# Third attention batch's loads moved to GpSimd's queue, behind the first expert's second weight matrix, with the front's order drawn up anew

## The chip, the core and the metric

The kernel runs on one core of one Trainium2 chip. The metric is the device time of one execution in microseconds (us). A core has five engines that run their own instruction lists side by side: TensorE (PE, matrix multiply), VectorE (DVE), ScalarE (ACT), GpSimd (POOL) and SyncE (SP, here only a queue that issues transfers). Transfers are issued either from SP or from GpSimd and are carried out by 16 DMA engines that all queues share.

## The reference, cut to what matters

Linear attention (8 batches, 8 heads, 576 positions, head width 64) makes the tokens, and a mixture of 8 experts works on them. The gate weights are normalised by eight Sinkhorn rounds over all 4608 tokens, so they are known only when the last batch is through attention.

```python
phi = lambda x: np.where(x > 0, x, np.exp(x) - 1.0) + 1.0
q_p, k_p = phi(q), phi(k)
kv  = einsum('bhsd,bhse->bhde', k_p, v);  z = sum(k_p, axis=2)
x   = einsum('bhsd,bhde->bhse', q_p, kv) / (einsum('bhsd,bhd->bhs', q_p, z) + 1e-6)
# x is laid out as N = 4608 tokens of D = 512
P = exp(x @ w_gate - max);  8 times: P /= row sums;  P /= column sums;  P *= N / E
for e in range(8):                       # F = 1024
    out += P[:, e:e+1] * (maximum(x @ w1[e], 0) @ w2[e])
```

## The kernel before

The kernel has a front and a long main part. The front (about the first 200 us) runs the attention of the 8 batches, two half batches `n = 2b + g` for each batch, and fills TensorE's gaps with expert 0, group by group of 512 tokens (`hq` is the first layer, `ye` the second). The main part runs experts 1 to 7 with a seven-product block scheme.

Nothing is ordered by hand. The program is a list of tasks; a small planner inside the kernel (`_Plan`) gives each engine a fixed order when the kernel is built. It uses written-in durations (here 6.0 for a whole weight matrix) and a table of priorities, `ranks`, which may also pin a copy to ACT or DVE. What the chip then executes is a fixed list for each engine.

The loads. A weight matrix is float32 in memory and is cast to float16 by the transfer; only GpSimd issues it:

```python
def load_w(ten, nm, pl, ap, cut, e, prio, parts=1, after=0.0, deps=()):
    ...
    for i in range(parts):
        def fn(_, i=i):
            ...                                     # part i of the matrix
            nc.gpsimd.dma_start(out=dst, in_=AP(tensor=ten.tensor, offset=off, ap=a))
        ti = add(("pool", 1.0), fn, use=[g], prio=prio, deps=[tal])
        ts_.append(add(("dma", 6.0 / parts), lambda _: None, deps=[ti], use=[g], prio=prio, lat=2.6))
        w_last[0] = ti
```

The inputs of a half batch (`k`, `q`, `v`, 576 KB each; two buffers for each of the three):

```python
for nm, ten in (("k", k), ("q", q), ("v", v)):
    def fn(_, gr=gr, nm=nm, ten=ten):
        gr["tile"] = fp.tile([P, 2, NJ, D], FP32, tag=nm + "in", name=nm + "in", bufs=2)
        (nc.gpsimd if n in (2, 3) else nc.sync).dma_start(...)
    ti = fadd(("pool", 1.0) if n in (2, 3) else ("sp", 0.45), fn, acq=[gr], prio=pr,
              deps=[w_last[0] if n in (2, 3, 4) else None, in_prev[0]])
...
att(0, 0); att(0, 1)
w_t = {0: load_w1(0, prio=-290.0, parts=2, deps=[gates[0]])}
for b in range(1, B):
    att(b, 0); att(b, 1)
    if b == 1:
        w_t[0] += load_w2(0, prio=-96.5, parts=2, deps=[in_prev[0]])
    if b % 2 == 1:
        logits(b // 2)
add(("pool", 0.8), f_wg, prio=-90.0, deps=[w_last[0]])     # w_gate, 8 KB
```

One half batch then runs: `ek`, `eq` (exponentials, ACT), `tk`, `tq` (DVE), `vv` (a cast, ACT or DVE), and on TensorE `kv_ps`, `qt_ps` (transposes of q), `den_ps`, `num_ps`, `xt_ps` (transposes of the result into `xT`), with DVE or ACT copies between them (`kvz`, `qpT`, `rden`, `xn`, `xT`). The small matrix products use one pair of PSUM buffers in turn (`att`).

The second layer of expert 0 needs one half of w2 for the first four of its eight products, the other for the last four:

```python
for half in range(2):
    for f in range(4 * half, 4 * half + 4):
        nc.tensor.matmul(gy[tt]["tile"], lhsT=gh["tile"][:, f, ds(P * tt, P)], rhs=gw2["tile"][:, f, :], ...)
    ty[tt] = add(("pe", 0.87), f_y, deps=[tw2[half], ty[tt]] + ..., ...)
```

In the built program GpSimd issues the half with rows `f` 4 to 7 first and the half with rows 0 to 3 second, before and after the change alike; TensorE wants rows 0 to 3 first.

At the start, 47 products on a tile of zeros (`yw <- warm`) keep TensorE occupied while there is no other work.

Of the kernel before, what the change touches and what calls it, by code (L numbers as in the profile page):

```python
# [122 lines left out]
def kernel(  # L123
# [10 lines left out]
    nc = tc.nc  # L134
# [17 lines left out]
    add = S_.add  # L152
# [41 lines left out]
    def load_w(ten, nm, pl, ap, cut, e, prio, parts=1, after=0.0, deps=()):  # L194
        g = S_.grp(pl)
        ts_ = []
# [4 lines left out]
        for i in range(parts):  # L201
            def fn(_, i=i):
                dst, a, off = g["tile"], [list(x) for x in ap], e * DM * F
                if parts > 1:
                    n = a[cut][1] // parts
                    off += i * n * a[cut][0]
                    a[cut][1] = n
                    dst = dst[:, i * n:(i + 1) * n, :] if cut == 1 else dst[:, :, i * n:(i + 1) * n]
                nc.gpsimd.dma_start(out=dst, in_=AP(tensor=ten.tensor, offset=off, ap=a))
            ti = add(("pool", 1.0), fn, use=[g], prio=prio, deps=[tal])  # L210
            ts_.append(add(("dma", 6.0 / parts), lambda _: None, deps=[ti], use=[g], prio=prio, lat=2.6))
            w_last[0] = ti
# [21 lines left out]
    def fadd(*a, **kw):  # L234
        t = add(*a, **kw)
        front_ids.append(t)
        return t

    def att(b, g):
        n = 2 * b + g  # L240
# [9 lines left out]
        for nm, ten in (("k", k), ("q", q), ("v", v)):  # L250
            gr = gin[nm] = S_.grp(p_in[nm])

            def fn(_, gr=gr, nm=nm, ten=ten):
                gr["tile"] = fp.tile([P, 2, NJ, D], FP32, tag=nm + "in", name=nm + "in", bufs=2)
                (nc.gpsimd if n in (2, 3) else nc.sync).dma_start(
                    out=gr["tile"].rearrange("p r j d -> p r (j d)"),
                    in_=AP(tensor=ten.tensor, offset=(b * H + 4 * g) * S * D, ap=src))
            ti = fadd(("pool", 1.0) if n in (2, 3) else ("sp", 0.45), fn, acq=[gr], prio=pr,
# [666 lines left out]
    for tt in (3, 2, 1, 0):  # L925
# [5 lines left out]
        0:8.9853 36:-98.0084 38:-98.0036 40:-98.021 42:-85.0117 43:-85.0126 44:-98.0219 45:-85.0096  # L931
        46:-98.0036 47:-98.0147 49:-85.0105:act 50:9.0018 51:-98.0201 52:-98.0087 54:-85.0123 55:9.0204:dve
        56:-85.0102 57:8.9967:dve 58:8.9967 59:-98.0183 61:-85.0111 62:8.9928 63:-98.0015 64:8.9928
        65:-98.0039 66:-85.0066 67:-85.0105 68:-85.0126:act 69:-85.0096 70:-98.0054:dve 71:-85.0081
        73:8.9976 75:-98.0006 77:-98.0015 78:-98.0204 79:-85.009 80:8.9946 81:-85.0117 82:-98
        84:-85.0111:dve 85:-98.0165 86:8.9991 88:9.0003 89:-85.0006 90:-85.0084 91:-85.0087:act 92:-98.0105
        93:8.9916 95:8.9934 96:8.9979 97:-98.0081 98:-85.0087 99:-98.018 100:-85.0105 101:-85.009
        102:-98.0054 103:-85.0072 104:-98.0195 106:-97.9991 108:8.9934 110:-98.0042 112:-98.0165 114:8.994
        116:-98.0081 117:-98.0366 118:-98.009 119:-85.0108 120:-98.0216 121:-85.009 123:-85.0108
        124:-98.0084 125:-85.0126 127:-98.0042 128:-98.0036:act 129:8.9928 130:-98.018:dve 131:-85.0117  # L940
        132:-98.003 134:-98.0072 135:-85.0099 136:-98.0153 137:9.0153 138:-85.0099 139:-98.0051 140:-98.0315
        141:-98.0021:dve 142:-98.0081 143:-98.0024 144:-98.0183 146:-85.0132 148:8.9991 150:-98.0072
        151:8.9952 152:9.0189 153:-85.0099 154:-85.0075 155:-98.0105 157:8.9925:act 158:-98.0336
        159:-85.0132 161:-98.0093 162:-85.0084 163:-98.0321 164:-98.0093 165:8.9889 166:-98.0081
        168:-85.0138 169:-98.0153 170:-98.0078 171:-98.0156 172:-98.0081 173:-98.0084 174:-98.0168
        175:-98.0327:act 176:-98.0123 177:-85.0105:act 179:-85.0102 181:-98.0045 183:8.9943 184:-98.0054
        185:-85.0141 187:-98.0096 189:8.9913 191:-98.0153 192:-98.0039 193:-85.0096 194:-98.0069 195:9.0174
        196:9.0192 198:8.9937 199:-98.0033 200:-85.0078 202:-85.0117 203:-98.0075:act 204:-98.0012
        205:-98.0222 206:-85.0147 207:-98.0111 209:-98.0243 210:-85.0132 211:7.6305 212:-85.0084 213:9.0072
        214:-98.0066 215:-98.015 216:-85.0084 217:-97.9949 218:-85.0078 219:-85.009 221:-85.0075  # L950
        223:-85.0081 225:-98.0177 226:8.9943 227:-98.0342 228:-85.0105 229:9.0192 230:-98.0081
        232:8.9934:act 233:-98.0102 234:-98.0069 236:-85.0132 237:-98.0339:dve 238:-85.0063 239:-98.0078:act
        240:-98.0063 241:8.9928 243:-85.0093 244:8.9907 245:8.9853 246:-98.0075 247:-98.015 248:-98.0357
        249:-98.0156 250:-85.0138 251:-98.0159 252:-85.0117 253:-98.009 255:-85.0111 257:-98.0099
        259:-98.0054 260:-98.0123 261:8.9916 262:-85.0135 263:-98.0054 264:8.9994 266:-98.009:dve 267:8.9931
        268:-98.0123 270:-85.0216 271:-98.0345:act 272:-85.0141 273:-85.009:act 274:-85.0078 275:-85.0129
        277:-98.015 278:-98.0108 279:8.9928 280:-98.0135 281:-98.0186 282:8.9904 283:8.9931 284:-85.0126:act
        285:-98.012 286:-85.0072:act 287:-98.0084 289:8.9952 291:-85.0066 293:-85.0099 294:-97.9958
        295:-85.0126 296:8.9892 297:-85.0072 298:-98.0051 300:8.9943:dve 301:-98.0138 302:8.9862
        304:-98.0156 305:-98.018 306:-85.0219 307:-98.012:act 308:-85.0099 309:8.9916 311:8.9859  # L960
        312:-98.0192 313:-98.0111 314:-85.0108 315:8.9913 316:8.9904 317:8.9952 318:-85.003:dve 319:-85.0099
        320:8.994:dve 321:-85.012 322:-85.0021 323:9.0195 325:-98.0327 327:-98.0249 329:-98.03 330:-85.0075
        331:9.0198 332:-98.0054 333:-85.0069 334:-98.0201 336:-98.0177:act 337:8.9874 338:-98.0108
        340:-85.0204 341:-85.0099 342:8.9925 343:8.9895 344:-85.0069 345:9.0078 347:-98.0222 348:-85.0126
        349:-85.0144 350:-85.0081 351:-98.0249 352:-85.0159 353:-98.0021 354:-98.0141:act 355:8.9874
        356:-98.015:act 357:9.0057 359:-85.0132 361:-85.0078 363:-85.0054 364:8.9889 365:-98.0114
        366:-85.006 367:-85.0156 368:-85.0093 370:8.9904:dve 371:9.0153 372:-85.0126 374:-85.0042 375:8.994
        376:8.9913 377:8.997:act 378:7.6314 379:-85.0114 381:8.9931 382:-85.0096 383:-98.0174 384:-85.012
        385:-98.0147 386:-85.0081 387:-98.0237 388:-85.0114:act 389:-98.0015 390:-98.0141:act 391:-98.0315
        393:-98.0222 395:8.9904 397:-98.0045 398:8.9985 399:-85.0135 400:-98.0168 401:8.9874 402:-85.0111  # L970
        404:-98.0138:act 405:8.9895 406:-97.9976 408:-85.0027 409:-85.0087:dve 410:-98.0024 411:-85.0087
        412:-85.0126 413:-98.0165 415:-98.0021 416:-85.012 417:-98.006 418:-98.0132 419:-85.0204 420:8.9952
        421:-98.0177 422:7.6257 423:-85.0102 424:-85.0117 425:-85.015 427:8.991 429:-85.0096 431:-98.021
        432:-98.0147 433:9.0138 434:8.9889 435:-85.0144 436:-85.0129 438:-98.0189:dve 439:-85.0105
        440:8.9904 442:-85.0081 443:-98.0015 444:-85.0108 445:-98.0069:dve 446:-85.012 447:-85.0111
        449:-85.0111 450:-85.0126 451:-85.0126 452:-85.0114 453:-98.0387 454:8.9859 455:-98.0054
        456:-98.0003:dve 457:-98.0132 458:-85.0096 459:7.6254 460:-98.0189 461:8.985 463:-85.0144
        465:-98.0045 467:8.9961 468:-85.0084 469:8.9877 470:-85.0135 471:-98.0273 472:-85.0144 474:8.9886
        475:-85.0138 476:-98.0072 478:-85.0129 479:-98.0288:act 480:7.6269 481:-97.9991 482:7.6263
        483:9.0102 485:7.6218 486:-97.9949 487:-98.0054 488:-98.0279 489:-85.0123 490:7.6281 491:-85.0129  # L980
        492:8.9913 493:7.6278 494:7.6203:act 495:-85.0147 497:-97.9979 499:-97.9991 501:8.9937 502:-98.0072
        503:-98.0246 504:-85.009 505:-98.0156 506:-85.0093 508:-98.0141 509:8.9877 510:8.9913 511:-98.0168
        513:-98.0138 514:8.9922 515:7.6248 516:7.6263 517:-85.0123 518:-97.9964 520:7.6206 521:-98.0138
        522:7.6269 523:-97.9967 524:-85.0135 525:-98.0063 526:-98.0045 527:-98.0039:dve 528:-98.0198
        529:-85.0087:dve 530:-85.0123 532:-98.0183 534:8.9859 536:-85.0129 537:-85.0129 538:-97.9946
        539:-85.0117 540:-85.012 541:-85.0087 543:-85.0108:act 544:-98.015 545:8.991 547:-98.0045
        548:-85.0114 549:-85.0114 550:8.9925 551:-85.012 552:7.6221 554:-98.0192 555:-98.0258 556:-97.9955
        557:7.6269 558:7.6251 559:7.6287 560:-85.0105 561:-85.0141 562:-85.0111 563:-98.0213 564:-85.0114
# [85 lines left out]
```

## Time and profile before

| what | value |
|---|---|
| time, median of 3 runs | 979.14 us (978.08 to 980.62) |
| profiled span | 978.4 us |
| TensorE busy | 960.5 us (98%) |
| VectorE busy | 765.9 us (78%) |
| ScalarE busy | 567.9 us (58%) |
| GpSimd busy | 111.0 us (11%) |
| mean granted TensorE clock | 0.994 |
| bytes moved | 121.97 MB |

The page of the profile gives the busy time of each engine, the span in 40 slices of about 24.5 us, the chain of work that ended last, the costliest groups of instructions, and the transfers with their median time from issue to landing. TensorE is at or near full in every slice but the second and the last, so the parts of the trace to look at are its few gaps. The trace also answers for a stretch of time: who waited for whom, the instructions of one engine in order, and the busy time, granted clock and transfer rate of each microsecond.

### The profile page before, as it was taken

To read this page: it belongs to the slowest core of one execution; us is meant where nothing else is said; L and a number is where in the kernel's file an instruction comes from. 1 tells how busy PE (TensorE), PEld (TensorE's weight loads), DVE (VectorE), ACT (ScalarE), POOL (GpSimd) and SP (SyncE) were. 2 spreads that over 40 slices of the span, in tenths; PEclk is the share of its full clock that TensorE was granted. 3 is DMA by queue.
4 is the path that set the end of the run, shared out by engine and by line. 5 is a ranking of instruction groups with operands and counts; after the bars stand their busy time and mean duration, and the time that the engine had idled before them with its cause. 6 is when DMAs were issued, how large, how long until landed. Compare 5 with 4: busy or idle time off the path is not lost.

```text
span 978.4 us, 21349 instructions
## 1 busy us (share of the span) xinstructions
PE 960.5 (98%) x8737; PEld 794.7 (81%) x8737; DVE 765.9 (78%) x1517; ACT 567.9 (58%) x1016; POOL 111.0 (11%) x158
## 2 busy tenths in 40 slices
PE   9699999999999999999999999999999999999998
PEld 4366565578888888888888888888888888888886
DVE  6497667897888788878888788878888788877775
ACT  5398654486555555555555555555555555555553
POOL 4000000001111111111111111111111111111110
PEclk9799999999999999999999999999999999999999
DMA  9788535762225422272225422272225422226554
GB/s 317 205 315 283 142 76 186 230 123 76 77 77 123 115 76 77 76 162 76 76 76 123 115 77 76 76 163 76 76 77 123 116 76 77 77 87 172 163 162 108
DMA packets 47186, 121.97 MB, mean 125 GB/s; under 512 B 4208, under 2 KB 18288, under 8 KB 47088
## 3 DMA queue, kind: packets, MB, share of 16 engines
q1 hardware_dynamic: 32208, 99.76, 30.7%
q0 software_dynamic: 14480, 20.33, 11.6%
q8 instruction: 68, 1.11, 0.5%
q10 hardware_dynamic: 400, 0.52, 0.2%
q14 instruction: 30, 0.25, 0.1%
HBM read 119.69 MB, written 17.69 MB: 140 GB/s over the span
## 4 chain that ended last, share of the span: by engine, by line
PE 91%; DMA 4%; ACT 3%; issue 0%; DVE 0%; SPq 0%; ACTq 0%; POOLq 0%
PE ye L839 32%; PE hq L633 22%; PE att L633 11%; PE ye L729 7%; PE Zye L633 5%; PE hq L539 5%; PE Zye L839 5%; DMA w<-in_moe_w_dram 3%; ACT acc L751 1%; PE xt_ps L381 1%; PE num_ps L365 1%; DMA vin<-in_v_dram 1%; PE kv_ps L303 1%; PE qt_ps L326 1%; ACT eq L268 0%
## 5 line engine op out<-in xcount | busy, mean ns | idle before, releaser
L853 DVE SCALAR_TENSOR_TENSOR acc<-ye,P_sb,acc 128x256 f32<-128x256 f32 x620 | 267.3, 480 | 127.4 <-PE ye L839 126.5
L633 PEld LDWEIGHTS <-W 128*128 128x128 f16 x2016 | 197.3, 98 | 24.3 <-issue 1.0
L839 PEld LDWEIGHTS <-S 128*128 128x128 f16 x1984 | 193.9, 98 | 23.8 <-DVE S L812 1.4
L839 PE MATMUL ye<-T,S 128*128 128x256 f16 x1488 | 192.8, 273 | 0.2 <-DVE S L812 0.2
L633 PEld LDWEIGHTS <-w 128*128 128x128 f16 x1512 | 147.9, 98 | 18.4 <-issue 0.5
L839 PEld LDWEIGHTS <-h 128*128 128x128 f16 x1488 | 145.6, 98 | 18.0 <-issue 1.2
L659 ACT ACTIVATE h<-hq 128x512 f16<-128x512 f32 x126 | 75.2, 597 | 144.5 <-PE hq L633 141.6
L863 POOL TENSOR_TENSOR acc<-acc,st 128x256 f32<-128x256 f32 x124 | 88.1, 730 | 622.8 <-ACT st L860 593.2
L633 PE MATMUL hq<-xs,W 128*128 128x256 f16 x1008 | 151.2, 273 | 0.7 <-ACT Zye L645 0.6
L633 PE MATMUL att<-xs,W 128*128 128x256 f16 x1008 | 151.2, 273 | 0.0
L633 PE MATMUL hq<-xs,w 128*128 128x256 f16 x1008 | 140.9, 273 | 0.3 <-DVE h L662 0.3
L656 ACT ACTIVATE h<-Zye 128x512 f16<-128x512 f32 x126 | 75.3, 598 | 40.3 <-PE Zye L633 40.3
L860 ACT ACTIVATE st<-Zye,P_sb 128x256 f32<-128x256 f32 x124 | 52.0, 471 | 75.5 <-PE Zye L839 75.5
L662 DVE CUSTOM_DVE_ANT_0 h<-att,s 128x512 f16<-128x512 f32 x126 | 86.6, 687 | 11.5 <-ACT s L649 10.8
L812 DVE TENSOR_TENSOR S<-h 128x1024 f16<-128x1024 f16 x124 | 85.2, 687 | 11.6 <-ACT h L659 11.6
L649 ACT COPY s<-hq 128x512 f32<-128x512 f32 x126 | 73.5, 583 | 35.7 <-PE hq L633 35.7
L662 DVE CUSTOM_DVE_ANT_0 h<-hq,s 128x512 f16<-128x512 f32 x126 | 86.6, 687 | 0.3
L729 PE MATMUL ye<-w,h 128*128 128x512 f16 x312 | 77.9, 387 | 8.8 <-DMA w<-in_moe_w_dram 8.8
L645 ACT COPY Zye<-hq 128x512 f32<-128x512 f32 x126 | 73.3, 582 | 16.0 <-PE hq L633 16.0
L633 PE MATMUL Zye<-xs,w 128*128 128x256 f16 x504 | 75.6, 273 | 0.0
L653 ACT COPY s<-att 128x512 f32<-128x512 f32 x126 | 74.6, 592 | 0.0
L539 PE MATMUL hq<-xT,w 128*128 128x512 f16 x288 | 70.6, 379 | 0.7 <-ACT h L543 0.3
(92 smaller groups left out, 943.3 us busy)
## 6 DMA issues: line engine op xcount, KB each, us to landing
xs<-xd SPq DMA_DIRECT2D x63, 896.0 KB, 4.6
w<-in_moe_w_dram POOLq DMA_DIRECT2D x14, 1024.0 KB, 10.2
out_dram<-acc SPq DMA_DIRECT2D x67, 128.0 KB, 2.4
kin<-in_k_dram SPq DMA_DIRECT2D x14, 576.0 KB, 6.3
qin<-in_q_dram SPq DMA_DIRECT2D x14, 576.0 KB, 6.2
vin<-in_v_dram SPq DMA_DIRECT2D x14, 576.0 KB, 6.5
xd<-xst SPq DMA_DIRECT2D x9, 512.0 KB, 2.7
xd<-xT SPq DMA_DIRECT2D x9, 256.0 KB, 3.5
```

The costliest lines, as they stand in the source:

```text
L539: nc.tensor.matmul(ghq["tile"], lhsT=gw1["tile"][:, c, ts(f, P)], rhs=xT[:, c, ds(512 * g, 512)], start=(c == 0), stop=(c == NDT - 1))
L633: nc.tensor.matmul(dst[:, p, :], lhsT=lhs(p, c), rhs=rhs(c), start=(first and p == 0 and c == 0), stop=(c == 1), skip_group_check=True)
L649: nc.scalar.copy(out=gs2["tile"], in_=gX["tile"])
L653: nc.scalar.copy(out=gs5["tile"], in_=gR["tile"])
L656: nc.scalar.activation(out=hd(0, 0), in_=Zt[1], func=AF.Relu)
L659: nc.scalar.activation(out=hd(1, 0), in_=gX["tile"], func=AF.Relu)
L662: nc.vector._custom_dve(TENSOR_ADD_SAT, out=dst, in0=ps, in1=sb, s0=3.0e38, s1=0.0)
L729: nc.tensor.matmul(gy[tt]["tile"], lhsT=gh["tile"][:, f, ds(P * tt, P)], rhs=gw2["tile"][:, f, :], start=(f == 0), stop=(f == NFT - 1))
L812: nc.vector.tensor_tensor(out=Sx[:, i], in0=a0, in1=a1, op=op)
L839: nc.tensor.matmul(bank(g_)[:, s, :], lhsT=lhs(s, kk), rhs=rhs(kk), start=(new and s == 0 and kk == 0), stop=(kk == 3), skip_group_check=True)
L853: nc.vector.scalar_tensor_tensor(out=dst(), in0=bank(g_)[:, s, :], scalar=P_sb[:, gg, e:e + 1], in1=dst(), op0=ALU.mult, op1=ALU.add)
L863: nc.gpsimd.tensor_tensor(out=dst(), in0=dst(), in1=gst["tile"], op=ALU.add)
```

## The change: what it does and what it is for

The loads of half batches `n` = 4 and 5 (the third batch) are issued by GpSimd instead of SP. GpSimd's queue then holds, in order, the two halves of w1, the inputs of the second batch, the two halves of w2 and the inputs of the third batch. Before, the third batch's loads stood in SP's queue, and could run beside those of w2. The aim is that w2 is not slowed by them. The planner's duration of a weight matrix goes from 6.0 to 5.3, and the table of priorities is new: 963 entries for 800, with a new order of the front and of the hand-over from expert 0 to expert 1.

```diff
-            ts_.append(add(("dma", 6.0 / parts), lambda _: None, deps=[ti], use=[g], prio=prio, lat=2.6))
+            ts_.append(add(("dma", 5.3 / parts), lambda _: None, deps=[ti], use=[g], prio=prio, lat=2.6))
...
-                (nc.gpsimd if n in (2, 3) else nc.sync).dma_start(
+                (nc.gpsimd if 2 <= n <= 5 else nc.sync).dma_start(
                     out=gr["tile"].rearrange("p r j d -> p r (j d)"),
                     in_=AP(tensor=ten.tensor, offset=(b * H + 4 * g) * S * D, ap=src))
-            ti = fadd(("pool", 1.0) if n in (2, 3) else ("sp", 0.45), fn, acq=[gr], prio=pr,
+            ti = fadd(("pool", 1.0) if 2 <= n <= 5 else ("sp", 0.45), fn, acq=[gr], prio=pr,
                       deps=[w_last[0] if n in (2, 3, 4) else None, in_prev[0]])
...
     ranks = """
-        0:8.9853 36:-98.0084 38:-98.0036 40:-98.021 42:-85.0117 43:-85.0126 44:-98.0219 45:-85.0096
... (the rest of the old table)
+        0:-394.9868 36:-395.0096 38:-395.0507 40:-395.0054 42:-397.9952 43:-397.9946 44:-394.9934
... (the rest of the new table)
```

What the two built programs' instruction lists show:

- TensorE has the same instructions in both, in another order through the front and the hand-over. The first `ye` stands after all eight `hq` blocks of group 0 and the `kv_ps` and `qt_ps` of both half batches of batch 1, in both. The new list has one more `num_ps` piece (four products) ahead of it.
- The new list asks for `kv_ps` of half batch 4 six `ye` blocks (of four products) after that point; its ACT list has `ek` of half batch 4 directly after the last `h` and `qpT` of that stage.
- GpSimd's list: `w1` half, `w1` half, six inputs of batch 1, `w2` half, then before: `w2` half, `w_gate`; after: `w_gate`, `w2` half, six inputs of batch 2. GpSimd's transfers take eight completion semaphores in turn, and each waits for the transfer that used its semaphore last; so the second `w2` half now waits for batch 1's first `k` where it waited for the second half of `w1`.
- From ACT to DVE go, over the whole front and hand-over, 3 + 2 `qpT` copies, 2 `xT` copies, 2 copies of `ye` and 7 scalings of the accumulator by the gate; one `vv` cast goes the other way.

## The prediction, made before the changed kernel was run

> **What bounds the kernel now.** I read the page first, then the chain of waits in order of time, then TensorE's own list around the break, then the stretches of one microsecond. Sections 1 and 4 of the page:
>
> ```profile
> PE 960.5 (98%) x8737; PEld 794.7 (81%) x8737; DVE 765.9 (78%) x1517; ACT 567.9 (58%) x1016; POOL 111.0 (11%) x158
> PE 91%; DMA 4%; ACT 3%; issue 0%; DVE 0%; SPq 0%; ACTq 0%; POOLq 0%
> ```
>
> TensorE is the bound: 960.5 of 978.4 us busy, so only 17.9 us of gaps can be won by any new order. The second line says that 4% of the span is a transfer. The chain in order of time (start, duration, what) tells which:
>
> ```profile
> 9.43 8.06 DMA w<-in_moe_w_dram
> 17.49 0.28 issue
> 17.77 21.96 DMA w<-in_moe_w_dram
> 39.73 0.04 issue
> 39.77 1.86 PE ye L729 x4
> ```
>
> One half of w2 is issued at 17.77 and lands 21.96 us later. TensorE's list at that place (start, duration, then in brackets the idle time before):
>
> ```profile
> 30.29 0.69 PE L303 MATMUL kv_ps<-vv,tk 64*128 64x130 f16 x18
> 39.77 1.86 PE L729 MATMUL ye<-w,h 128*128 128x512 f16 x4 [8.79 <-DMA w<-in_moe_w_dram]
> ```
>
> So TensorE stands for 8.79 us, half of all its gaps, for this one landing. Why does it take 21.96 us? The lists of the two issuing engines:
>
> ```profile
> 15.55 0.76 POOL L209 DMA_DIRECT2D w<-in_moe_w_dram  x1
> 17.77 0.75 POOL L209 DMA_DIRECT2D w<-in_moe_w_dram  x1 [1.47 <-DMA w<-in_moe_w_dram]
> 20.27 1.01 POOL L466 DMA_DIRECT2D wg_sb<-in_moe_w_gate_dram  x1 [1.75 <-DMA kin<-in_k_dram]
> ```
>
> ```profile
> 21.30 0.37 SPq L255 DMA_DIRECT2D kin<-in_k_dram  x1
> 23.33 0.37 SPq L255 DMA_DIRECT2D qin<-in_q_dram  x1
> 23.86 0.37 SPq L255 DMA_DIRECT2D vin<-in_v_dram  x1
> 25.77 0.37 SPq L255 DMA_DIRECT2D kin<-in_k_dram  x1
> ```
>
> Four of the third batch's six loads are in SP's queue by 25.8 us, while w2 still stands behind batch 1's inputs in GpSimd's. The single-microsecond windows (busy time of PE, PEld, DVE, ACT, POOL, then granted clock, transfer share, GB/s) show the price:
>
> ```profile
> 30.00:31.00 1.00, 0.98 (x23) 0.79 (x23) 0.19 (x1) 0.99 (x2) 0.00 (x0) 1.00 1.12 294
> 35.00:36.00 1.00, 0.00 (x0) 0.00 (x0) 0.00 (x0) 0.00 (x0) 0.00 (x0) 0.67 1.12 297
> 36.00:37.00 1.00, 0.00 (x0) 0.00 (x0) 0.00 (x0) 0.00 (x0) 0.00 (x0) 0.50 1.14 299
> 40.00:41.00 1.00, 1.00 (x3) 0.29 (x2) 0.00 (x0) 0.00 (x0) 0.00 (x0) 0.50 0.69 186
> 45.00:46.00 1.00, 1.00 (x6) 0.46 (x5) 0.28 (x1) 0.00 (x0) 0.00 (x0) 0.71 0.00 0
> ```
>
> The DMA engines are full while every compute engine stands. And the clock falls to 0.5 in the stall: 0.67 over microsecond 35 puts the fall at 35.34, and 0.71 over microsecond 45 puts the return at 45.58. TensorE restarts at 39.77 and runs 5.81 us at half speed.
>
> **What the Trainium skill says.** *DMA: Bandwidth & Descriptors*, section "Queues, rings and completion order": each DMA engine goes round the queues that have work, a packet from each in turn. The trace agrees. By issue plus time to landing, batch 1's inputs, alone on GpSimd's queue, land at 20.0, 21.5, 23.0 and 24.5, that is 1.5 us each; once SP's queue is moving, the same transfers land at 26.2 and 28.5. The two halves of w1, alone, land 2.56 us apart (14.93 and 17.49); those of w2, in company, 5.6 us apart (34.1 and 39.73). *TensorE: Matmul & The Clock Gate*, section "What's actually happening": the clock is granted by a free-running window of 3.413 us; an idle window halves it, a busy one restores it. The trace fits: fall and return are 10.24 us apart, three such windows. The same page ("Step-by-step: what each phase is for") says that matmuls stay in program order; here nothing behind `ye` ran during the stall.
>
> **The change, part by part.**
>
> *Step 1: landing of w2.* After the change no other queue has work until w2 is through, as the next SP load (half batch 6) needs a buffer that half batch 4 has to use first. From `kin` at 24.5 the two inputs behind it take 1.5 each: 27.5. First half of w2 at the rate of w1's halves: 30.1. Then `w_gate`, which now stands before the second half. It landed at 20.27 + 22.0 = 42.3, 2.5 after w2 and in company; alone I put it at 1.0 (an estimate, between 0.7 and 1.3). Second half: 30.1 + 1.0 + 2.56 = **33.6**. It is issued later (it waits for a `kin` that landed at 20.0), but long before its turn. So the first `ye` starts at about 33.65 instead of 39.77: **6.1 us** earlier. All of it is on the path, if TensorE is there by then. It was there at 30.98; the new list has one more `num_ps` piece ahead (four products, 0.23) and DVE work between (`vv`, `rden`, `xn` of 0.28 to 0.75 each) that frees PSUM for the last `qt_ps`, so I put it at 31.5 to 32.2.
>
> *Step 2: the clock.* The gap shrinks from 8.79 to some 1.5 to 2.2 us, which can't hold a whole idle window of 3.41. In the trace, a window with TensorE idle for its last part only (to 31.93, of which 0.95 idle) kept the clock. So the clock should stay at 1.0, and half of 5.81 us, **2.9 us**, is saved. Over runs the phase differs: return needs one full window, so this saving is 1.7 to 3.4.
>
> *Step 3: the third batch's inputs come later.* They queue behind w2, at 1.5 each: k 35.1, q 36.6, v 38.1, then 39.6, 41.1, 42.6. Before they landed at 29.1 to 42.1. Who needs them first? `kv_ps` of half batch 4 stands behind six `ye` blocks (0.86 each from the chain at full clock, 5.2), one `den_ps` (0.24), `num_ps` pieces (0.7) and four `xt_ps` (1.1): 7.2 us after the restart, at 40.9. Its `vv`, on ACT, waits for v at 38.1 and for `eq` before it (`ek` 1.17, two copies of 0.6, `eq` 1.17 from 35.1: 38.7), so it is ready at about 39.9. It is in time by 1 us; the second half batch's `v` (42.6) has some 6 us more of work ahead of it. So the delay is nearly hidden. But ACT and DVE are close to full there: in the five windows of 5 us from 50 to 75 us before, DVE is busy 4.45 to 4.96 of 5. They lose the quiet time that TensorE's slow clock gave them, and the `att` PSUM pair, freed by them, then holds TensorE for moments (before, gaps of this kind at 15 to 31 us were 0.14 to 0.27 each). I put four or five such gaps: **0.9 us lost**.
>
> *Step 4: the hand-over.* Between 209 and 227 us TensorE has five gaps of 0.20 to 0.62, 2.2 in all, that wait for ACT's copies and DVE's `S`; ACT is full in that stretch:
>
> ```profile
> 205.00:215.00 10.00, 9.48 (x81) 7.70 (x80) 9.63 (x22) 10.00 (x20) 2.30 (x3) 1.00 0.94 195
> ```
>
> The new order moves seven scalings of about 0.5 us from ACT to DVE, but DVE has only 0.4 of 10 us free. I put **0.5 us gained**, with 1 us either way. The 760 us after it do not change.
>
> The sum: 979.14 - 6.1 - 2.9 + 0.9 - 0.5 = **970.5 us**, 0.9% faster.
>
> **The rivals.** (a) *A later landing takes the stall's place*: TensorE waits for `kv_ps` of half batch 4 or 5 instead of w2. For it speaks that these inputs land up to 6 us later on a path with 1 us of slack; against it, the new list was drawn up with this queue in it. If each is 2 us late: 974.5. (b) *VectorE becomes the bound of the front*: it sat idle for 10.65 us in the old stall and can't win back more than it has room for. DVE has 5.6 to 8.4 of 10 us busy from 80 to 140, so a debt would be paid off by about 100 us, but TensorE could lose 2 to 3 us by then: 972.5 to 973.5. (c) *The stall stays long enough for the clock to fall*: if w2's slowest engine is late by 2 us more, the gap is near 4 us and the clock may fall; then 2.0 more wait and up to 2.9 of clock: 975.4. (d) *The load was hidden anyway*: the 8.79 us wait rules it out. For the better side: with no stall at all and a clean hand-over, 979.14 - 8.8 - 2.9 - 2.2 = 965.2 is the floor.
>
> **Range and chances.** Centre 970.5; the rivals reach to 975.4, and the floor is 965.2, of which I trust all but 1.3. I take 966.5 to 976.0. To be 2% faster it would need 959.6, below the floor; 2% slower is 998.7, for which no part of the change has the means. Chances: 0.01 faster, 0.98 within, 0.01 slower.
>
> **What would show it.** Step 1: the first `ye` of expert 0 starts near 33.6 and its wait for w2 is 1 to 3 us. Step 2: the granted clock is 1.00 in every microsecond from 5 to 900. Step 3: the third batch's loads are in GpSimd's list, landing 35 to 43; between 34 and 80 TensorE has gaps of under 1 us each, about 0.9 in sum. Step 4: gaps of about 1.7 us between 200 and 230. I am wrong if TensorE waits over 2 us at one `kv_ps` or `qt_ps` of batch 2, if the w2 wait is over 3.4 us with the clock at 0.5 behind it, or if a gap opens in the Sinkhorn and hand-over part that was not there.

## The result, and the profile after

The changed kernel takes **968.85 us** (median of 4 runs, 968.27 to 969.96), the kernel before, on the same chip, 979.88 (median of 4, 978.08 to 980.63). The ratio is 0.9891, with a 95% interval of 0.9874 to 0.9909: 1.1% faster, and inside the predicted range (966.5 to 976.0) on the better side of its centre (970.5).

Busy times and the chain's shares, sections 1 and 4 of the page of the changed kernel:

```profile
PE 957.1 (99%) x8737; PEld 794.1 (82%) x8737; DVE 771.1 (80%) x1532; ACT 560.8 (58%) x1001; POOL 115.1 (12%) x164
PE 94%; DMA 3%; ACT 2%; issue 0%; DVE 0%; ACTq 0%
```

TensorE's share of the chain that sets the end rises from 91 to 94%. Its gaps longer than 0.06 us, without the 1.3 us ahead of its first product, add up to 4.2 us; they were 12.5. The chain in order of time (start, duration, what) still goes through w2, but through less of it:

```profile
20.27 12.09 DMA w<-in_moe_w_dram
32.36 0.04 issue
32.40 1.02 PE ye L729 x4
```

The second half of w2 is issued 2.5 us later than before and lands 7.4 us earlier. GpSimd's list shows why (start, duration, transfer, then the idle time before it):

```profile
17.74 0.75 POOL L466 DMA_DIRECT2D wg_sb<-in_moe_w_gate_dram  x1 [1.78 <-DMA w<-in_moe_w_dram]
20.27 0.80 POOL L209 DMA_DIRECT2D w<-in_moe_w_dram  x1 [1.78 <-DMA kin<-in_k_dram]
21.92 1.06 POOL L255 DMA_DIRECT2D kin<-in_k_dram  x1 [0.84 <-DVE xT L225]
30.24 0.72 POOL L255 DMA_DIRECT2D vin<-in_v_dram  x1 [1.17 <-DVE xn L370]
```

The third batch's loads, 21.92 to 30.24, stand in the same queue behind w2, and all six are issued before w2's second half lands at 32.36. SP issues its next load only at 36.58. TensorE's list at the old break, and the two single-microsecond windows around it (busy time of PE, PEld, DVE, ACT, POOL, then granted clock, transfer share, GB/s):

```profile
30.98 0.67 PE L326 MATMUL qt_ps<-ident,tq 128*128 128x128 f16 x9
32.40 1.02 PE L729 MATMUL ye<-w,h 128*128 128x512 f16 x4 [0.76 <-DMA w<-in_moe_w_dram]
...
39.75 0.69 PE L303 MATMUL kv_ps<-vv,tk 64*128 64x130 f16 x18
```

```profile
31.00:32.00 1.00, 0.65 (x10) 0.53 (x9) 0.33 (x2) 0.82 (x2) 0.00 (x0) 1.00 1.02 391
32.00:33.00 1.00, 0.60 (x3) 0.29 (x3) 0.11 (x1) 0.36 (x1) 0.00 (x0) 1.00 1.00 405
```

The wait for w2 falls from 8.79 to 0.76 us, the clock stays at 1.00, and `kv_ps` of half batch 4, the first reader of a delayed input, has no wait in its line at all. The hand-over has no gap left. The hand-over now comes some 10 us earlier, so the window that answers to before's from 205 to 215 us (ACT 10.00, DVE 9.63 of 10 us) is this one of the changed kernel:

```profile
195.00:205.00 10.00, 10.00 (x90) 8.58 (x88) 8.92 (x17) 5.30 (x11) 2.29 (x3) 1.00 0.58 140
```

One gap behind the restart is new. TensorE's line, and the waits between 20 and 140 us that lead to it (who waited for whom: total us, times, longest):

```profile
106.16 0.42 PE L341 MATMUL den_ps<-kvz,qpT 128*128 128x2 f16 x10 [1.42 <-DVE qpT L225]
```

```profile
ACT eq L268 <- DMA qin<-in_q_dram: 2.9, 2, 2.7
DVE tq L272 <- DMA qin<-in_q_dram: 2.1, 1, 2.1
PE den_ps L341 <- DVE qpT L225: 1.4, 1, 1.4
```

Read from below: `den_ps` of the last half batch waits for `qpT`, a copy of the transposes of `tq`, and `tq` and `eq` wait for the last `q`. SP issued that `q` at 94.95, and it took 9.9 us to land, against 4.9 for the `q` before it. At 94.38 GpSimd had issued expert 1's first weight matrix, which landed 13.5 us later. It is the removed fault over again, with the parts exchanged: here a weight load on GpSimd's queue slows an input on SP's.

Ahead of the restart the new order also has two longer gaps, where before the longest was 0.27 us:

```profile
21.19 1.17 PE L539 MATMUL hq<-xT,w 128*128 128x512 f16 x4 [0.64 <-DVE xT L225]
23.12 1.89 PE L539 MATMUL hq<-xT,w 128*128 128x512 f16 x8 [0.76 <-ACT h L543]
```

They cost nothing here, since TensorE still waits for w2 behind them. They count as soon as that wait is gone.

From the hand-over to the end, the two profiles run 11.8 us apart without change, so the whole gain is made before about 230 us. By the profile pair: first `ye` 39.77 to 32.40, 7.4; the clock 2.7 (the shift that is left between the before profile and the filled stall below, where the wait is the same); the new gap -1.4 and another at 181 us, `ye` behind a copy of ACT, -0.3; four `num_ps` products now done ahead, 0.2; what remains, 3.2, falls to the hand-over, 2.2 of it the five gaps. The profiled execution of before was 1 us slower than its median, so the medians (11.0 apart) give each term a little less.

### The profile page after: what moved, and what is told of

It is laid out like the page before. It is cut to its first block, busy times and chain, and to the rows that moved or that the text cites. A ratio compares the mean times of both kernels' runs of the same rounds, so it can differ in the third digit from the quotient of the medians.

```text
span 966.5 us, 21349 instructions
## 1 busy us (share of the span) xinstructions
PE 957.1 (99%) x8737; PEld 794.1 (82%) x8737; DVE 771.1 (80%) x1532; ACT 560.8 (58%) x1001; POOL 115.1 (12%) x164
## 3 DMA queue, kind: packets, MB, share of 16 engines
q1 hardware_dynamic: 30576, 96.22, 29.9%
## 4 chain that ended last, share of the span: by engine, by line
PE 94%; DMA 3%; ACT 2%; issue 0%; DVE 0%; ACTq 0%
PE ye L839 33%; PE hq L633 23%; PE att L633 11%; PE ye L729 6%; PE Zye L633 6%; PE Zye L839 6%; PE hq L539 5%; DMA w<-in_moe_w_dram 1%; DMA kin<-in_k_dram 1%; DMA qin<-in_q_dram 1%; PE yw L472 1%; PE xt_ps L381 1%; PE num_ps L365 1%; PE kv_ps L303 1%; PE qt_ps L326 1%; ACT acc L751 0%
```

## The experiments

The theories. **Queue**: the move of six loads makes the gain, as it keeps transfers away from w2. **Order**: the new table makes it, by giving TensorE other work, and the loads are incidental. Within the queue theory there are two rivals for how it works: w2 is *isolated* (any queue would do), or the delayed inputs must also come *at once* behind it. And the clock's part was to be measured by itself.

### The queue alone

The kernel before, with only the loads moved; TensorE's, DVE's and ACT's lists stay as before.

```diff
-                (nc.gpsimd if n in (2, 3) else nc.sync).dma_start(
+                (nc.gpsimd if 2 <= n <= 5 else nc.sync).dma_start(
-            ti = fadd(("pool", 1.0) if n in (2, 3) else ("sp", 0.45), fn, ...
+            ti = fadd(("pool", 1.0) if 2 <= n <= 5 else ("sp", 0.45), fn, ...
```

> The kernel before with the third batch's six loads issued by GpSimd behind w2, old priorities. TensorE's, DVE's and ACT's lists stay those of before, so this is the queue alone. Theory A (the queue carries the gain): both halves of w2 land near 32.4 us as in the changed kernel, the first ye starts at 32.5 instead of 39.77, its wait is 1.5 us, the clock stays 1.0: 7.3 + 2.9 us gained, 1 us lost to a list that was not drawn up for the later inputs, so 970 to 972 us. Theory B (the new order carries it, the queue only lets it): the old lists run into late inputs of the third batch, a wait of 3 us or more appears at a kv_ps, and the time is 975 us or more.

Measured: 971.01 us (median of 5, 970.80 to 973.31), ratio 0.9918 (0.9905 to 0.9930). TensorE's line at the break, and the window of the hand-over:

```profile
32.77 1.02 PE L729 MATMUL ye<-w,h 128*128 128x512 f16 x4 [1.31 <-DMA w<-in_moe_w_dram]
```

```profile
205.00:215.00 10.00, 8.86 (x77) 7.18 (x75) 8.61 (x18) 10.00 (x20) 0.00 (x0) 1.00 0.29 98
```

8.2 us of the gain are the queue's: `ye` 7.0 us earlier, and the clock. The hand-over keeps its five gaps of the same lengths, 10 us earlier. The halves of w2 land at 30.05 and 32.72, 2.67 apart, with `w_gate` behind both of them.

### The order alone

The changed kernel, with `n in (2, 3)` put back in both lines; TensorE's, DVE's and ACT's lists stay as in the changed kernel.

```diff
-                (nc.gpsimd if 2 <= n <= 5 else nc.sync).dma_start(
+                (nc.gpsimd if n in (2, 3) else nc.sync).dma_start(
-            ti = fadd(("pool", 1.0) if 2 <= n <= 5 else ("sp", 0.45), fn, ...
+            ti = fadd(("pool", 1.0) if n in (2, 3) else ("sp", 0.45), fn, ...
```

> The changed kernel with the third batch's six loads back on SP's queue. TensorE's, DVE's and ACT's lists stay those of the changed kernel, so this is the new order alone. Theory A: w2 lands near 39.7 us again, the first ye waits about 8 us, the clock falls to 0.5 and returns near 45; what is left is the hand-over without gaps (1.9 us): 976.5 to 978.5 us. Theory B: 972 us or less.

Measured: 980.61 us (median of 17, 980.12 to 983.29), ratio 1.0017 (1.0010 to 1.0024): slower than before, and above the range of theory A too. Out of its chain in order of time, and TensorE's list:

```profile
20.09 21.77 DMA w<-in_moe_w_dram
```

```profile
41.90 1.44 PE L729 MATMUL ye<-w,h 128*128 128x512 f16 x3 [10.28 <-DMA w<-in_moe_w_dram]
```

Without the queue the stall is back, and is 1.5 us longer. By issue and time to landing, w2's first half lands at 33.65, `w_gate`, which now stands between the halves, at 36.99 and the second half at 41.86: the halves are 8.2 us apart, where they were 5.6 in the kernel before. The clock is at 0.5 from 36.21 to 46.45. The hand-over is clean (TensorE 10.00 of 10 us in all four windows from 195 to 235), but the longer stall and a gap of 1.65 at `den_ps` near 116 us outweigh that. The order theory falls as a cause of its own. But the parts don't simply add up: the order costs 1.4 us without the queue, and gains about 2.2 with it (971.01 to 968.85, not on one chip). Most of the difference lies at the break: the new order brings w2's second half 2.1 us later than before without the queue (41.86 against 39.73), and 0.4 earlier with it (32.36 against 32.72).

### What the clock is worth

The kernel before, with products on the tile of zeros in the stall, into the accumulator that the first `ye` then starts afresh. Nothing else moves, and the wait for w2 stays.

```diff
+                    if e == 0 and g == 0 and tt == 0 and half == 0:
+                        for _ in range(38):         # or 33, or 28
+                            nc.tensor.matmul(gy[tt]["tile"], lhsT=warm[:, 0:P], rhs=warm, start=True, stop=True)
```

> The kernel before with 38 products of the tile of zeros put in front of the first ye block (into the PSUM tile that this block then overwrites), 8.2 us at full clock, so inside the stall. Loads and lists else as before. If the slow clock costs what the prediction says, the clock stays at 1.0, w2 still lands at 39.7, and the time falls by 1.7 to 3.4 us, 2.9 in the middle: about 977. Rival: after the stall DVE and ACT set the pace and the half-speed stretch was hidden: no change, 979.5 to 980.

Measured: 977.78 us (median of 18, 977.23 to 978.35), ratio 0.9984 (0.9977 to 0.9991). The 38 products ran from 32.09 to past 40.3, 0.6 us beyond w2's landing at 39.67, and so took back part of what the clock gave. Hence 33 products:

> As the filling of the stall with 38 products, but 33: with 38 they ran to 40.30, 0.6 us beyond w2's landing. 33 end at about 39.2. The clock stays 1.0, the first ye starts at 39.7, and the time is 0.5 us under that of the 38: 977.2, or 2.0 under before.

Measured: 977.43 us (median of 14, 977.09 to 978.01), ratio 0.9983 (0.9975 to 0.9991). The products end at 38.26, 1.53 us before `ye`, and the clock is at 1.0 from there on. The saving is 1.6 us by the medians (979.02 to 977.43), 2.7 by the profile pair: before's mean granted clock was 0.994 in some of its runs and 0.997 in others, and its profile is one with 0.994. To see how long a gap the clock bears, 28 products:

> As the filling with 33 products, but 28: TensorE then stands for about 2.6 us before w2 lands, less than one clock window of 3.41. If the clock falls only after a window that is idle throughout, as the prediction had it, it stays at 1.0 in every run and the time is that of 33 products, 977.4. If a window that is half idle is enough (2.13 us at 38.0 in one of the runs above, 1.67 and 1.70 at 104 and 110 in two others were followed by a fall), it falls in about three of four runs, by where the windows lie, those runs have a mean clock of 0.998 and are 1 to 1.7 us longer: median 978.5.

Measured: 977.54 us (median of 13, 976.49 to 979.34), ratio 0.9981 (0.9973 to 0.9989). TensorE's line:

```profile
39.56 1.02 PE L732 MATMUL ye<-w,h 128*128 128x512 f16 x4 [2.63 <-DMA w<-in_moe_w_dram]
```

A gap of 2.63 us, and the clock was still 1.00 in the microseconds that follow. That does not show that half an idle window is harmless, since the gap was split. In each trace the changes of the clock lie on one grid of 3.413 us (in the isolation run below: 40.19, 43.60, 111.87 and 115.28). In this one the clock falls behind the last product at 976.87, and 275 steps back from there a window ends at 38.20, inside the gap: 1.27 us of it lie in one window, 1.36 in the next. In one of the 13 runs the mean clock was 0.998 and the time 979.34, so there it presumably fell. How long the gap was in the other twelve, and where their windows lay, is not on record.

### Rows 0 to 3 of w2 first

The half that TensorE wants first is issued first; the changed kernel otherwise.

```diff
+                    i = parts - 1 - i if cut == 1 else i
```

> The changed kernel with the two halves of w2 exchanged in GpSimd's queue: rows 0 to 3, which the first ye needs, go first and land near 29.9 us, rows 4 to 7 near 32.4 us. All lists stay. If the remaining wait of 0.76 us is on the path: the wait is gone, the first ye starts at 31.65, 968.1 us. Rival: the vector work behind it takes it back, and the time stays 968.8.

Measured: 969.07 us (median of 4, 967.98 to 969.81), ratio 0.9892 (0.9878 to 0.9905): no change. The wait for w2 is gone and the first `ye` starts at 32.02, but the gap at `den_ps` is 1.67 in place of 1.42, and in this run the clock fell behind it, from 106.86 to 110.28. In this profile the first `ye` is only 0.4 us earlier than in the changed kernel's, as the gaps at 21 and 23 us are 0.9 longer in sum; at 105 us 1.9 are lost, of which the clock is 1.7.

### Isolation without the queue

The changed kernel, with the third batch's loads back on SP, and ahead of them a small transfer that reads rows 0 to 3 of w2 (128 x 8 elements into a scratch tile in memory). SP so holds them back until w2 is in.

```diff
+                if n == 4 and nm == "k":
+                    nc.sync.dma_start(out=scr, in_=w_t[0][2]["tile"][:, 0, 0:8])
-                (nc.gpsimd if 2 <= n <= 5 else nc.sync).dma_start(
+                (nc.gpsimd if n in (2, 3) else nc.sync).dma_start(
```

> The changed kernel with the third batch's loads back on SP's queue, but SP first stores 2 KB of w2's rows 0 to 3 to a scratch tensor, so it waits for w2 to land before it issues them. No load runs beside w2, and GpSimd's queue doesn't hold the inputs. If what counts is that nothing runs beside w2, and not whose queue it is: w2 lands at 32.4 as in the changed kernel, the clock stays 1.0, and the inputs land about 2.5 us later than there (k at 36.4, v at 39.4), so that kv_ps of half batch 4 waits 1 to 1.5 us: 970 us. If GpSimd's queue itself is what helps: 976 or more.

Measured: 975.08 us (median of 5, 974.62 to 975.62), ratio 0.9957 (0.9945 to 0.9970). That is 5 us more than was expected. w2 was nearly as early as it should be (first `ye` at 33.12, wait 0.72; the changed kernel has 32.40 and 0.76). The waits of this kernel between 34 and 45 us:

```profile
ACT ek L271 <- DMA kin<-in_k_dram: 5.9, 1, 5.9
...
DVE tk L275 <- DMA kin<-in_k_dram: 2.4, 1, 2.4
PE num_ps L368 <- DVE xT L226: 2.1, 1, 2.1
```

SP issues `k` at 33.57, and `ek` can start at 39.03; in the changed kernel it starts at 34.02, since there the same load was long issued and came 1.6 us behind w2. ACT and DVE take their lists in order: DVE runs `tk` at 38.97, and only behind it, at 39.65, the copy `xT` that TensorE's `num_ps` waits for. TensorE stands 2.13 us there, and the clock is at 0.5 from 40.19 to 43.60 and once more from 111.87 to 115.28. A mean clock of 0.996 or 0.997 fits two falls in each of the five runs. So the inputs' delay is *not* harmless: 5 us more of it breaks the path. It breaks through DVE's list, though, and not at `kv_ps`, as the prediction's rival (a) had it; `kv_ps` of half batch 4 has no wait here.

How much of the 5 us is the price of a queue in which nothing stands ready, the run does not settle. This `k` took 5.4 us to land, while SP's loads took 3.85 (`k` at 90.81 us in the kernel before) and 3.99 (`q` at 94.11 in the order alone), also with others directly behind them. Its transfer starts slowly behind the store, as two windows show (the last figure is GB/s):

```profile
36.00:37.00 1.00, 1.00 (x14) 0.76 (x13) 0.56 (x1) 0.00 (x0) 0.00 (x0) 1.00 0.49 35
38.00:39.00 1.00, 0.02 (x1) 0.00 (x0) 0.03 (x1) 0.00 (x0) 0.00 (x0) 1.00 1.06 415
```

And `k` is issued 0.5 us after w2's landing at 33.08, as the store goes first. These two, 1.4 and 0.5 us, may belong to the detour and not to SP's queue. Without them TensorE's wait would be about 0.2 us and the fall behind it would not come, which gives some 971.5 us (an estimate: 1.9 us less of wait, 1.7 of clock). So isolation alone brings w2 in early, and a `k` 5 us late takes a good part of that back: 3.9 us of gain are left. That the inputs must stand ready in the same queue is not shown.

### Expert 1's w1 behind the last inputs

The changed kernel, with the first weight load of expert 1 held until the last half batch's `v` is in (`gates[15]`); w2 is held behind it.

```diff
-    w_t[1] = load_w1(1, prio=0.0, deps=[gates[13]]) + load_w2(1, prio=0.0, deps=[gates[15]])
+    w_t[1] = load_w1(1, prio=0.0, deps=[gates[13], gates[15]]) + load_w2(1, prio=0.0, deps=[gates[15], w_last[0]])
```

> The changed kernel with expert 1's first matrix (1024 KB as written, issued at 94.4 us, beside the last half batch's q at 95.0, which takes 9.9 us to land) held back until the last half batch's v has landed. Engine lists stay, but for the place of one gate copy and one load on GpSimd. If that transfer is what stops TensorE for 1.42 us at 104.7, the gap is gone, the q lands in under 6 us, and the time falls by 1.4 to 2: 967.2. Rival (VectorE is behind at that place, not the transfer): the gap stays at over 1 us and the time stays 968.8.

Measured: 966.93 us (median of 4, 966.46 to 967.20), ratio 0.9874 (0.9859 to 0.9889). The last `q` lands 6.6 us after its issue in place of 9.9, the last `v` 6.6 in place of 11.6, and `den_ps` doesn't wait. GpSimd's list has both weight loads together, 9 us later:

```profile
103.78 1.64 POOL L209 DMA_DIRECT2D w<-in_moe_w_dram  x2
```

That is early enough for expert 1: the hand-over stays without a gap. With the halves of w2 exchanged as well:

> Both: expert 1's first matrix behind the last inputs, and the halves of w2 exchanged. Exchanging the halves alone gave nothing that can be told from the changed kernel, as other waits before the first ye grew by as much; so 967.2, as with the first edit alone. If the exchange was only hidden by the gap at 104.7: 966.5.

Measured: 966.22 us (median of 4, 965.65 to 966.36), ratio 0.9865 (0.9851 to 0.9878). On the same chip the exchange now gives 0.7 us by the medians of four runs each, which don't overlap; while the gap at 105 us stood behind it, it gave nothing. In the pair of profiles it gives 0.1, as the gaps at 21 and 23 us, which are now on the path, are 0.8 us longer in one than in the other.

### Changed and best side by side

> The changed kernel unaltered, for a comparison on the same chip with the best version: 968.9.

> Expert 1's first matrix behind the last inputs and the halves of w2 exchanged, unaltered, beside the changed kernel: 966.2, 2.5 us less than it.

Measured on one chip, beside before at 979.26 (median of 17): changed 969.67 us (median of 4, 968.56 to 970.49), ratio 0.9902 (0.9888 to 0.9915); with both edits 966.13 (median of 4, 965.88 to 966.24), ratio 0.9866 (0.9853 to 0.9880). So 3.5 us are still to be had, with no overlap of the runs. Of the changed kernel's four, two have a mean clock of 1.0 (968.56, 968.96) and two of 0.998 (970.38, 970.49). The profile is one of the latter, and two of its windows show where:

```profile
107.00:108.00 1.00, 0.96 (x12) 0.47 (x9) 1.00 (x3) 0.21 (x1) 0.00 (x0) 0.85 0.23 51
108.00:109.00 1.00, 1.00 (x4) 0.36 (x3) 0.96 (x4) 0.48 (x1) 0.19 (x1) 0.50 0.00 0
```

The gap at `den_ps` is 1.72 us in this execution, and the clock is at 0.5 from 107.71 to 111.12, which is one window of 3.41 us. Half of that, 1.7, is the distance between the two pairs of runs. In all four runs of the version with both edits the clock is 1.0.

## Why the prediction was right, and where its steps were not

**The bound and the main mechanism** held. TensorE's wait for one half of w2 was the cost, and the queue alone takes most of it away (8.2 of 11 us). That the two queues shared the engines packet by packet can be counted in the kernel before, from 28 to 36 us (queue: packets, MB, share of the 16 engines; q1 is SP's, q0 GpSimd's):

```profile
q1 hardware_dynamic: 731, 1.59, 58.3%
q0 software_dynamic: 729, 0.73, 53.7%
```

**Step 1, landing of w2: right, one term too large.** Put at 33.65, it was 32.40; TensorE was there at 31.65, inside the 31.5 to 32.2. The term that failed is `w_gate`, put at 1.0 us. By issue and time to landing, w2's rows 4 to 7 land at 29.7, `w_gate` at 29.9 and rows 0 to 3 at 32.36. The halves are 2.67 apart, and they are 2.67 apart with the queue alone too, where `w_gate` does not stand between them; so 8 KB in a queue without company cost nothing that these runs can show. In company it is another matter: 2.5 us behind w2 in the kernel before, 3.3 behind the first half in the order alone. The first half was also 0.4 us earlier than put.

**Step 2, the clock: right in outcome, too large in size, and its rule not safe.** The clock stays up at 32 us. Its worth was put at 2.9 us (1.7 to 3.4); the filled stall measured 1.6 by the medians, as the profile that was read belonged to a run in which the loss was large. That "the granted clock is 1.00 in every microsecond from 5 to 900" is false in some executions, by the gap at 105 us. And the argument that a short gap "can't hold a whole idle window" fails as a rule: the clock fell behind gaps of 2.13 us (isolation, fall at 40.19), 1.72 (changed kernel side by side, 107.71), 1.70 (isolation, 111.87) and 1.67 (halves exchanged, 106.86), each of which lay whole in one window of the grid. The skill's page *TensorE: Matmul & The Clock Gate*, section "What's actually happening", has the fall "after ≥1 idle window"; these runs fit its window of 3.413 us in the grid of the changes and in the length of the falls (3.41 or 10.24), but not in what starts one. A gap of 1.65 us that lay whole in one window (order alone, to 117.96) was not followed by a fall, nor was the one of 2.63 us that the grid split into 1.27 and 1.36. So where a gap lies in the grid matters, and about half a window of idle time was enough. That is not yet a safe border: behind the last products, windows idle for 1.71 and 1.78 us (filled stall with 33 and 28) kept the clock, and a gap of 2.63 us would by this border keep it only where the grid splits it near its middle, while one of the 13 runs shows the loss. Whether what runs in the rest of the window counts too stays open.

**Step 3, the inputs' delay: right that it is hidden, wrong about the price.** `kv_ps` of half batch 4 started at 39.75, put at 40.9, without a wait, and between 34 and 80 us TensorE has no gap where 0.9 us of small ones were put. The isolation experiment shows that the margin is finite: with `k` 5 us later TensorE stands 2.13 us, by way of DVE's list. The loss came elsewhere and for another reason. The 1.42 us at 105 us (and 1.7 more where the clock follows) come from expert 1's w1 beside the last `q`; the prediction named a new gap only for the Sinkhorn part and the hand-over and for batch 2's products, and looked for no second weight load that shares the time with an input.

**Step 4, the hand-over: too small.** Put at 0.5 us, all five gaps went, 2.2 us, and by difference some 3.2. The step weighed DVE's room in one window against seven scalings of 0.5 us. In the changed kernel the window that answers to it has ACT at 5.30 and DVE at 8.92 of 10: both became lighter, so work was spread over time, which a count of moved instructions can't show.

**The sum** was 8.6 us of gain for a measured 11.0. Gains that were put too low (1.3 of landing beyond the estimate, 0.9 of small gaps that did not come, 2.7 of hand-over) outweigh a clock that was put too high by 1.3, a gap of 1.4 to 3.1 (with the clock) that was not seen, and the 0.3 at 181 us. It is near the truth partly since these offset each other. Of the rivals, (d) and (c) fell by the run itself, (b) left no gap between 34 and 80 us, and (a) did not occur: no `kv_ps` of batch 2 waits, not even in the isolation run, where the inputs came later still and TensorE stood at `num_ps`.

## What to carry to other kernels

Before a critical load is moved, look at what runs beside it. Putting what is wanted next in the same queue behind it worked here: it then neither slows the load nor has to be issued after it. Another way to keep the load alone may do as well, if the next loads don't come later by it; here one such way made `k` 5 us later, and 3.9 us of gain were left of the changed kernel's 11.0. After such a change, look for the next place where a weight load and an input meet, since the same fault was worth 3.5 us more here, together with the order of w2's halves. A new instruction order should be tried together with the queue it was drawn up for, and not be judged alone.

## What the runs showed of the hardware

- With work on two queues the DMA engines took as many packets from one as from the other: 731 of SP's queue and 729 of GpSimd's from 28 to 36 us in the kernel before.
- A transfer of 8 KB between two weight halves of one queue, without company, could not be seen in their distance (2.67 us apart with it and without it). With another queue at work it landed 3.3 us behind the half before it.
- Loads that stand ready in a queue follow at 1.5 to 1.6 us each. Issued by SP, with others directly behind, a first load was there 3.85 to 3.99 us after its issue, and 5.4 us in the isolation run.
- Products on zeros kept the granted clock at 1.00 through 6 to 8 us of the old stall.
- The clock changed on a grid of 3.413 us. A fall was 3.41 us long where work resumed soon, and cost 1.7 us. Gaps of 1.67 to 2.13 us that lay whole in one window of the grid were followed by one; a gap of 1.65 was not, nor one of 2.63 that the grid split.
